# Seven half-block products for the down projection of the third and fourth batches

## The chip, the cores and the metric

The kernel runs on one core of one Trainium2 chip. The metric is the device time of one execution in microseconds (us). Before the change the median of three runs is 677.57 us (676.94 to 678.1). The program has the core's five engines: PE (TensorE, matrix products), DVE (VectorE), ACT (ScalarE), POOL (GpSimd) and SP (SyncE, which issues the transfers).

## The reference

Four batches go through a local attention with block summaries, and then through a mixer over tokens and channels. Cut to what matters:

```
attn: 4 batches, 8 heads, 768 tokens, 64 per head; softmax over a window of 16
      around each token and over 24 block maxima, times values and block means
x  = attention output, 768 tokens x 512 channels per batch
u  = x + (x^T U V)^T                    # token mixing, rank 32
ch = max(u @ w_ch1, 0) @ w_ch2          # 512 -> 2048 -> 512
return u + ch                           # float32
```

The change concerns `@ w_ch2`, called *down* below; `@ w_ch1` is called *up*.

## The kernel before

**Accuracy by parts.** Every factor of a large product is split into a high part (a cast by ACT) and a low part (value minus high part, by DVE or POOL); the function `split` does both. A product is then three matmuls: high by high, high by low, low by high.

**Batches.** The first batch is computed together with the preparation of the weights, by a list written out by hand. For the later three batches the kernel walks up and then down. Up is done by seven products of half blocks in place of eight (Strassen's scheme, in Winograd's form): the channels, the hidden units and the tokens are halved, sums of the weight blocks lie ready in memory (`up_there`), sums of the token blocks are made by `operands`, and `up_phase` makes, for each of 8 pairs of hidden blocks, seven products of 6 matmuls with 384 columns. Down is plain: `down_phase` goes over 16 hidden blocks `f`, and for each over 6 token tiles `t`, with three matmuls of 512 columns. There the activations are the stationary operand, so the result comes out in token rows and is added to `st.x`; later `finish` turns it by 24 transposes per batch into channel rows, which are what is stored.

**The work beside the products.** `gates` makes the high part (ACT, with the relu) and the low part (DVE, line 1136) of the 768 tokens of a hidden block, one block ahead. Weights come from memory whole: `fetch_weight` loads 512 KB at a time into a ring of three buffers, and `prepare` makes a *unit* of it, ACT the high part (line 184) and POOL the low part (line 185), into a ring of eight. About four units are ready ahead of their use. `tick` counts the steps until the next load, and `drip` issues small sums for the attention's block means.

**The order.** Each engine runs its instructions in the order in which the Python code emits them. The loop at the end of the body emits, after each step of up or down, the next pieces of the attention of the following batch (`later_steps`, spread evenly by `spread`), the finishing of the batch before (`finish`), a load when one is due, and a drip. In a step of up there are 6 matmuls, in a step of down 3.

Of the kernel before, what the change touches and what calls it, by code (L numbers as in the profile page):

```python
# [10 lines left out]
F32 = mybir.dt.float32  # L11
# [7 lines left out]
P = 128  # L19
# [25 lines left out]
BLOCKS = ("A11", "A12", "S2", "S1", "S3", "S4", "A22")  # L45
OPS = ("B11", "B21", "B22", "T1", "T2", "T3", "T4")
# [38 lines left out]
def body(ctx: ExitStack, tc, q0, q1, k, v, vn, uv, w1, w2, mask, ident, rep, out):  # L85
# [28 lines left out]
    def hidden_place(k, dt=F32):  # L114
        return wt.tile([P, 4 * NH], dt, name="place", tag=f"h{k}")
# [121 lines left out]
    def load_vsum(st, g, i):  # L237
# [4 lines left out]
        if st.b == 1 or st.b == 2 and g == 0:  # L242
            spare = hidden_place(2 + i)
        st.vn[g, i] = []
        for j in range(parts):
            if st.b == 0:
                t = vn0[g, i]
            elif spare is not None:
                t = spare[:, j * n : (j + 1) * n]
            else:  # L250
                t = mo.tile([P, DM], F32, name="stage", tag="val", bufs=VALS)[:, :n]
# [332 lines left out]
    def mix_u_out(st, hf, c):  # L584
        if hf not in st.u:
            st.u[hf] = [
                hidden_place(4 + 2 * hf + i, F32R).rearrange("p (c q) -> p c q", q=NH) for i in range(2)
# [3 lines left out]
        nc.scalar.copy(uh[:, c, :], ps[:, :NH])  # L591
        nc.vector.tensor_tensor(ul[:, c, :], ps[:, :NH], f32(uh)[:, c, :], ALU.subtract)  # L592
# [21 lines left out]

    def operands(st, i, k):

        if not st.op:
            for j, name in enumerate(OPS):
                t = wt.tile([P, 4 * NH], F32R, name="op", tag=f"op{j}")
                st.op[name] = t.rearrange("p (s i q) -> p s i q", s=2, q=NH)  # L620
        ps = turn_tokens(st, k < 2, 2 * i + k % 2)

        def part(name, val):
            t = st.op[name][:, :, i]
# [4 lines left out]

        if k == 0:  # L630
            st.tmp["T1"] = tmp()
            nc.scalar.copy(st.tmp["T1"], ps)
        elif k == 1:
            part("B22", ps)
            st.tmp["T3"] = tmp()
            nc.vector.tensor_tensor(st.tmp["T3"], ps, st.tmp["T1"], ALU.subtract)
            part("T3", st.tmp["T3"])
        elif k == 2:
            part("B11", ps)
            st.tmp["T2"] = tmp()  # L640
            nc.vector.tensor_tensor(st.tmp["T1"], st.tmp["T1"], ps, ALU.subtract)
            nc.vector.tensor_tensor(st.tmp["T2"], st.tmp["T3"], ps, ALU.add)
            part("T1", st.tmp["T1"])
            part("T2", st.tmp["T2"])
        else:
            part("B21", ps)
            nc.vector.tensor_tensor(st.tmp["T3"], ps, st.tmp["T2"], ALU.subtract)
            part("T4", st.tmp["T3"])
# [50 lines left out]
    down_there = [dram.tile([P, 2, DM], F32, name=f"down{p}", bufs=1) for p in range(NF // 2)]  # L699
# [608 lines left out]
```

## Time and profile before

The profiled execution took 678.02 us, of which 676.2 us lie between its first and last instruction (the span). The times are in us; each row is a stretch of the span. "Up" and "down" are those of the second, third and fourth batch.

| stretch | what | length | PE busy | DVE | ACT | POOL |
|---|---|---|---|---|---|---|
| 0 to 234 | first batch, weights, attention of the second | 234.0 | 208.7 | 176.1 | 117.6 | 157.1 |
| 234 to 306.5 | second, up | 72.5 | 70.7 | 45.4 | 45.9 | 45.8 |
| 306.5 to 386.5 | second, down | 80.0 | 79.1 | 45.3 | 35.7 | 31.8 |
| 386.5 to 462 | third, up | 75.5 | 74.9 | 40.2 | 50.7 | 50.8 |
| 462 to 542 | third, down | 80.0 | 79.1 | 43.3 | 35.7 | 27.6 |
| 542 to 601 | fourth, up | 59.0 | 59.0 | 15.5 | 34.1 | 37.9 |
| 601 to 669.3 | fourth, down | 68.3 | 68.3 | 20.6 | 20.3 | 21.1 |
| 669.3 to 676.2 | end: transposes, copies, stores | 6.9 | 2.2 | 0.4 | 3.2 | 0 |

A busy PE is a PE with a matmul in its pipeline. A recorded duration of an instruction on DVE or POOL contains what it waited inside the instruction. Rows of the timeline read: start, duration, engine, line, operation, output and inputs, shapes, count.

### The profile page before, as it was taken

What the parts mean: (1) busy time and instruction counts of PE and PEld (TensorE: products, weight loads), DVE (VectorE), ACT (ScalarE), POOL (GpSimd) and SP (SyncE); (2) the same over time, 40 slices, a digit from 0 to 9 for tenths busy, and PEclk for the clock granted to TensorE, in tenths of its full rate; (3) what the DMA queues carried; (4) which work ended last, traced back from release to release, by engine and by line L of the source; (5) the groups of instructions that cost most, each with busy time, mean ns of one, the idle gap of its engine ahead of it and who ended that gap; (6) DMA issues with size and microseconds to landing.
All of it is one profiled execution on the core that took longest, in us unless ns stands there. A gap on an engine that the chain in (4) does not pass through costs nothing.

```text
span 676.2 us, 13190 instructions
## 1 busy us (share of the span) xinstructions
PE 641.9 (95%) x4800; PEld 568.2 (84%) x4800; DVE 386.6 (57%) x1041; ACT 343.1 (51%) x751; POOL 372.0 (55%) x428
## 2 busy tenths in 40 slices
PE   5889997989999899999999999999999999999997
PEld 4768796879888799998877899998877899998886
DVE  3778798777898666555655634566654432232222
ACT  3855356355433556665453467665543365553322
POOL 5846967635697757651245486661334375563420
PEclk9999999899999999999999999999999999999999
DMA  9999679898992169785438059777432144431002
GB/s 250 249 345 279 218 231 297 252 272 305 279 330 100 52 185 309 209 250 151 143 104 248 23 174 311 229 222 220 127 97 79 55 148 165 139 126 62 32 0 94
DMA packets 82752, 124.47 MB, mean 184 GB/s; under 512 B 7680, under 2 KB 57728, under 8 KB 82688
## 3 DMA queue, kind: packets, MB, share of 16 engines
q1 hardware_dynamic: 82688, 123.63, 60.3%
q8 instruction: 38, 0.62, 0.4%
q14 instruction: 26, 0.21, 0.1%
HBM read 96.34 MB, written 27.26 MB: 183 GB/s over the span
## 4 chain that ended last, share of the span: by engine, by line
PE 75%; DMA 11%; DVE 6%; ACT 3%; SPq 2%; POOL 2%; issue 1%; ACTq 0%; POOLq 0%; DVEq 0%
PE acc L1151 27%; PE ps_h L1066 24%; PE acc L813 7%; PE ps_h L791 6%; PE ps_s L321 4%; PE ps_x L423 3%; DMA place<-in_q 2%; DMA qz<-in_q 2%; PE ps_o L610 2%; DMA place<-in_w 1%; DMA at<-there 1%; DMA place<-in_v 1%; DVE gl L1136 1%; DMA kt<-in_k 1%; DMA place<-in_k 1%
## 5 line engine op out<-in xcount | busy, mean ns | idle before, releaser
L185 POOL TENSOR_TENSOR parts<-whole,parts 128x512 fp32r<-128x512 f32 (+1 forms) x144 | 181.6, 1270 | 165.6 <-ACT parts L184 137.1
L1151 PE MATMUL acc<-parts,gh 128*128 128x512 f32 x576 | 193.4, 399 | 0.0
L1066 PE MATMUL ps_h<-op,parts 128*128 128x384 f32 x1008 | 188.4, 339 | 1.2 <-POOL parts L185 0.6
L1066 PEld LDWEIGHTS ps_h<-op,parts 128*128 128x128 f32 x1008 | 173.6, 188 | 3.1 <-POOL parts L185 0.9
L1151 PEld LDWEIGHTS acc<-parts,gh 128*128 128x128 f32 x576 | 108.1, 188 | 22.9 <-issue 0.8
L1151 PE MATMUL acc<-parts,gl 128*128 128x512 f32 x288 | 113.1, 393 | 1.9 <-DVE gl L1136 1.9
L1136 DVE SCALAR_TENSOR_TENSOR gl<-place,gh 128x768 fp32r<-128x768 f32 x48 | 58.9, 1228 | 83.1 <-ACT gh L1135 83.0
L184 ACT CAST parts<-whole 128x512 fp32r<-128x512 f32 (+1 forms) x144 | 83.5, 583 | 5.8 <-DMA whole<-up 4.3
L351 ACT ACTIVATE e<-e,neg 128x120 f32<-128x120 f32 x144 | 46.5, 386 | 59.7 <-DVE neg L341 53.6
L791 PE MATMUL ps_h<-place 128*128 128x384 f32 x384 | 74.3, 341 | 1.2 <-DVE place L592 0.5
L813 PE MATMUL acc<-place,gh 128*128 128x512 f32 x192 | 68.3, 411 | 2.1 <-POOL place L185 2.1
L791 PEld LDWEIGHTS ps_h<-place 128*128 128x128 f32 x384 | 66.6, 188 | 4.2 <-DVE place L592 1.3
L1135 ACT ACTIVATE gh<-place 128x768 fp32r<-128x768 f32 x48 | 40.6, 846 | 55.1 <-PE acc L1151 54.9
L1151 PEld LDWEIGHTS acc<-parts,gl 128*128 128x128 f32 x288 | 54.2, 188 | 13.1 <-DVE gl L1136 3.9
L160 POOL TENSOR_SCALAR val<-place 128x512 f32<-128x512 f32 (+1 forms) x30 | 48.7, 1638 | 29.6 <-ACT place L147 17.7
L185 POOL TENSOR_TENSOR place<-val,place 128x512 fp32r<-128x512 f32 x29 | 38.6, 1351 | 19.5 <-ACT place L184 19.5
L185 POOL TENSOR_TENSOR op<-tmp,op 128x384 fp32r<-128x384 f32 x24 | 24.5, 1030 | 42.7 <-ACT op L184 38.5
L341 DVE CUSTOM_DVE_ANT_0 e<-ps_s,mask_sb 128x120 f32<-128x120 f32 x144 | 32.9, 278 | 25.3 <-PE ps_s L321 24.5
L813 PEld LDWEIGHTS acc<-place,gh 128*128 128x128 f32 x192 | 36.6, 192 | 11.1 <-POOL place L185 3.4
L803 ACT ACTIVATE gh<-ps_h 128x384 fp32r<-128x384 f32 x32 | 15.6, 488 | 54.3 <-PE ps_h L791 54.1
L321 PEld LDWEIGHTS ps_s<-kt,qz 128*128 128x128 f32 x288 | 39.0, 191 | 4.4 <-DVE kt L303 1.6
L321 PE MATMUL ps_s<-kt,qz 128*128 128x120 f32 x288 | 39.7, 274 | 2.0 <-DVE kt L303 1.2
(110 smaller groups left out, 848.4 us busy)
## 6 DMA issues: line engine op xcount, KB each, us to landing
place<-in_w SPq DMA_DIRECT2D x32, 512.0 KB, 6.0
whole<-up SPq DMA_DIRECT2D x24, 512.0 KB, 4.0
whole<-down SPq DMA_DIRECT2D x24, 512.0 KB, 3.7
there<-squares SPq DMA_DIRECT2D x24, 384.0 KB, 4.2
at<-there SPq DMA_DIRECT2D x96, 96.0 KB, 3.9
whole<-up SPq DMA_DIRECT2D x24, 384.0 KB, 3.5
vt<-in_v SPq DMA_DIRECT2D x48, 146.2 KB, 4.0
kt<-in_k SPq DMA_DIRECT2D x24, 288.0 KB, 5.6
```

Of the source, the lines that this page charges most:

```text
L160: nc.gpsimd.tensor_scalar(f32(bits), f32(hi), 0.0, None, ALU.mult)
L184: nc.scalar.copy(hi, val)
L185: engine.tensor_tensor(lo, val, f32(hi), ALU.subtract)
L321: nc.tensor.matmul(ps[:, i * KC : (i + 1) * KC], qt[:, 64 + j * P : 64 + j * P + P], kt[:, k0 : k0 + KC], start=True, stop=True,)
L341: nc.vector.tensor_tensor_reduce(out=e[:, i, :], in0=ps[:, i * KC : (i + 1) * KC], in1=mask_sb[:, m, :], scale=-SCALE, scalar=BIG, op0=ALU ...
L351: nc.scalar.activation(e[:, i, :], e[:, i, :], AF.Exp, bias=st.neg[h][:, u : u + 1], scale=-1.0,)
L791: nc.tensor.matmul(ps[:, :NH], w_split[0, f][:, c % 2, part_w, c // 2], ut[:, c, :], start=(n == 0), stop=(n == 3 * NC - 1),)
L813: nc.tensor.matmul(acc[t], gt[:, sl], w_split[1, f][:, part_w], start=(first and j == 0), stop=(last and j == 2),)
L1066: nc.tensor.matmul(ps, a[:, sa, i], b[:, sb, i], start=(first and n == 0), stop=(n == 5), skip_group_check=not first,)
L1135: nc.scalar.activation(gh, h, AF.Relu)
L1136: nc.vector.scalar_tensor_tensor(gl, h, 0.0, f32(gh), ALU.max, ALU.subtract)
L1151: nc.tensor.matmul(acc[t], gt[:, sl], w[:, part_w], start=(f == 0 and j == 0), stop=(f == NF - 1 and j == 2),)
```

## The change

For the third and fourth batches (`st.b >= STRASSEN`, which is 2) down is done by seven products as well. `down_products` takes the products one after the other, each over all 8 pairs of hidden blocks: 56 steps of 6 matmuls with 384 columns. The weights are now the stationary operand, so the result comes out in channel rows; `sum_out` adds it on DVE to what is already there, and stores it. There is no `finish` for these batches; `operands` copies the turned tokens back into `st.x` (ACT), so that the mixed input stands in channel rows too.

The seven products need sums of activation blocks. Part of them is made in `up_phase` (one more relu on ACT and one more operation on DVE per pair), part in `part_steps`, which for each of the 56 steps makes the sum if there is one (DVE), the high part (ACT) and the low part (DVE, or POOL for some steps). It runs 7 steps ahead of the products. The sums of the down weights are made once, in the second batch's down, by `sum_down` (two operations on POOL and two on DVE for each of 8 pairs, and two stores), and loaded from `sums_there`. The third and fourth batches load 14 times 512 KB for down in place of 8 times, and prepare 28 units in place of 16.

The attention pieces move: 20 in place of 15 of the third batch's are issued in the second batch's up, the rest in the first 66 steps of its down; the fourth batch's first 8 steps are issued at the end of the second batch's down, the others in the third batch's up. Loads for the block means of the fourth batch start earlier. The sums of up weights of the first batch lie in two buffers and are stored in two transfers in place of one.

```
+PRODUCTS = (("A11", "x"), ("S1", "y"), ("S2", "x"), ("S4", "y"), ("S3", "x"), ("A12", "z"), ("A22", "x"))
+BLOCK_OF = (((0, 0),), ((1, 1),), ((0, 1),), ((0, 1),), ((1, 1),), ((0, 0),), ((1, 0),))
+STRASSEN = 2
...
+    def sum_down(p, whole):
...
+        yield nc.gpsimd.tensor_tensor(s12[:, 0], a21, a22, ALU.add)
+        yield nc.gpsimd.tensor_tensor(s12[:, 1], s12[:, 0], a11, ALU.subtract)
+        yield nc.vector.tensor_tensor(s34[:, 0], a11, a21, ALU.subtract)
+        yield nc.vector.tensor_tensor(s34[:, 1], a12, s12[:, 1], ALU.subtract)
+        yield
+        yield
+        yield nc.sync.dma_start(out=sums_there[:, :2, p], in_=s12)
+        yield nc.sync.dma_start(out=sums_there[:, 2:, p], in_=s34)
...
+    def part_steps(st, parts, n):
...
+        if n < steps:
+            j, b11, t1, b21, b22 = blocks(n)
+            if j == 2:
+                nc.vector.scalar_tensor_tensor(t1, b22, 0.0, t1, ALU.max, ALU.subtract)
+            elif j == 3:
+                nc.vector.tensor_tensor(b11, t1, b11, ALU.subtract)
+            elif j == 6:
+                nc.vector.scalar_tensor_tensor(b21, b21, 0.0, t1, ALU.max, ALU.subtract)
+        if 1 <= n <= steps:
...
+            if j in (3, 5):
+                nc.scalar.activation(hi, val, AF.Relu)
+            else:
+                nc.scalar.copy(hi, val)
...
+        if 2 <= n <= steps + 1:
...
+            if j in (3, 5):
+                nc.vector.scalar_tensor_tensor(lo, val, 0.0, f32(hi), ALU.max, ALU.subtract)
+            else:
+                engine = nc.gpsimd if n % 4 == 2 and (n < 24 or st.b == B - 1) else nc.vector
+                engine.tensor_tensor(lo, val, f32(hi), ALU.subtract)
+
+    def sum_out(st, j, i, ps):
...
+        u = channels_of(st, n, c)
+        if j < 3:
+            nc.vector.tensor_tensor(u, u, by_tiles(ps), ALU.add)
+            return
+        o = mo.tile([P, DM], F32, name="o", tag="val", bufs=VALS)[:, :NH]
+        nc.vector.tensor_tensor(by_tiles(o), u, by_tiles(ps), ALU.add)
+        t0 = st.b * S + n * NH
+        nc.sync.dma_start(out=out[c, :, t0 : t0 + NH], in_=o)
+
+    def down_products(st, parts):
...
+            for sa, sb in ((0, 0), (0, 1), (1, 0)):
+                for i in range(2):
+                    col = n % 2 * 2 * P + i * P
+                    nc.tensor.matmul(
+                        banks[name][i],
+                        w[:, sa, col : col + P],
+                        g[sb],
...
+            for _ in range(2):
+                if ahead <= n + LEAD:
+                    part_steps(st, parts, ahead)
+                    ahead += 1
+            if outs:
+                sum_out(*outs.pop(0))
+            if p == NF // 2 - 1:
+                outs = [(st, j, i, banks[name][i]) for i in range(2)]
+            if n % 2 == 1:
+                prepare()
+            yield
...
+    LEAD, FIRST_PARTS = 7, 5
...
-    do(behind)
```

On the engines the change shows at two places. The first is DVE in the fourth batch's down. Before (line 1136 is the low part of a gate; line 1092, 1126 are sums of up; line 1159 adds a result to the tokens; one row for 14 blocks):

```order
L1136 SCALAR_TENSOR_TENSOR gl<-place,gh 128x768
L1092 TENSOR_TENSOR place<-place,ps_h 128x384
L1126 TENSOR_TENSOR place<-place,ps_h 128x384
L1136 SCALAR_TENSOR_TENSOR gl<-place,gh 128x768
L1092 TENSOR_TENSOR place<-place,ps_h 128x384
L1136 SCALAR_TENSOR_TENSOR gl<-place,gh 128x768 x14
L1159 TENSOR_TENSOR x<-x,acc_7189 128x512
```

In the changed kernel, from the end of its second product on (line 1301 adds a product's result, line 1274 makes a sum of activation blocks, lines 1293 and 1290 make the low parts; `place` are the activation blocks, `op`, `gh` and `gl` the parts):

```order
L1301 TENSOR_TENSOR x_5194<-x_5194,accy0_7641 128x3x128
L1274 TENSOR_TENSOR place_6961<-place_6962,place_6961 128x384
L1293 TENSOR_TENSOR op_7745<-place_7379,op_7745 128x384
L1301 TENSOR_TENSOR x_5194<-x_5194,accy1_7642 128x3x128
L1274 TENSOR_TENSOR place_7016<-place_7017,place_7016 128x384
L1293 TENSOR_TENSOR op_7745<-place_7451,op_7745 128x384
L1274 TENSOR_TENSOR place_7090<-place_7091,place_7090 128x384
L1290 SCALAR_TENSOR_TENSOR gh_7769<-place_6961,gh_7769 128x384
L1274 TENSOR_TENSOR place_7162<-place_7163,place_7162 128x384
L1290 SCALAR_TENSOR_TENSOR gl_7781<-place_7016,gl_7781 128x384
```

Where one operation of 768 columns stood for each of 16 blocks, two of 384 columns stand for each step in such a stretch, and one elsewhere.

The second place is POOL in the third batch's down. Before (line 185 is the low part: `parts` of a weight unit, `op` of the next batch's token sums; `e` is a buffer of the attention):

```order
L336 MEMSET e_6010 128x8
L185 TENSOR_TENSOR parts_6034<-whole_5710,parts_6034 128x512
L185 TENSOR_TENSOR parts_6077<-whole_5777,parts_6077 128x512
L185 TENSOR_TENSOR parts_6146<-whole_5777,parts_6146 128x512
L185 TENSOR_TENSOR op_6138<-tmp_6189,op_6138 128x384
L185 TENSOR_TENSOR parts_6193<-whole_5970,parts_6193 128x512
L185 TENSOR_TENSOR op_6136<-tmp_6144,op_6136 128x384
```

In the changed kernel, from the start of that down (line 195 is `split`, line 1293 the low part of a step's activations):

```order
L1293 TENSOR_TENSOR gh_6130<-place_5025,gh_6130 128x384
L195 TENSOR_TENSOR parts_6150<-whole_6043,parts_6150 128x512
L195 TENSOR_TENSOR parts_6168<-whole_6043,parts_6168 128x512
L1293 TENSOR_TENSOR op_6184<-place_5624,op_6184 128x384
L195 TENSOR_TENSOR parts_6207<-whole_6102,parts_6207 128x512
L1293 TENSOR_TENSOR gh_6216<-place_5026,gh_6216 128x384
L195 TENSOR_TENSOR parts_6238<-whole_6102,parts_6238 128x512
```

One low part of activations now stands for every two units in the first product's steps, and there are 28 units in that down in place of 16.

More of the change, by code (lines that the diff above doesn't have):

```diff
@@ L768, in prepare @@
         prepared.append((key, t))
+        sums = second and key[0] == "down" and n < PER_BATCH
+        if sums:
+            stages.append(sum_down(key[1] // 2, fetched[n // 2]))
         if second:
-            due.append(4)
+            due.append(8 if sums else 4)
     def tick():
@@ L777, in tick @@
             fetch_weight()
+        if stages and next(stages[0], stages) is stages:
+            stages.pop(0)
     def use_weight(*key):
@@ L1186, in body @@
         cur, ahead, after = ([*sts, None, None][b + i] for i in range(3))
-        todo = later_steps(ahead) if ahead else []
-        mine, theirs = todo[:FIRST_STEPS], todo[FIRST_STEPS:]
-        steps = spread(mine, 4, UP)
-        ends = spread(behind, 2, 2 + 2 * len(behind))
+        new = b >= STRASSEN
+        todo = later_steps(ahead) if ahead and not new else []
+        if ahead and new:
+            steps = spread([(later_step, ahead, i) for i in range(EARLY, STEPS)], 9, UP)
+        else:
+            steps = spread(todo[:FIRST_STEPS], 4, UP)
+        ends = spread(behind, 2 - new, 2 - new + (2 - new) * len(behind))
         phase = up_phase(cur)
+        g = {}
         for i in itertools.count():
```

224 lines of the change are left out of this document (168 added, 56 removed).

## The prediction, made before the changed kernel ran

> **What bounds the kernel now.** I read the page first, then the busy times by stretch, then the chain of work that ended last. Page, busy times; and by stretch (length, then PE, PEld, DVE, ACT, POOL busy, with counts):
>
> ```profile
> PE 641.9 (95%) x4800; PEld 568.2 (84%) x4800; DVE 386.6 (57%) x1041; ACT 343.1 (51%) x751; POOL 372.0 (55%) x428
> ```
> ```profile
> 462.00:542.00 80.00, 79.07 (x632) 63.53 (x631) 43.30 (x92) 35.69 (x70) 27.58 (x24) 1.00 0.34 102
> 542.00:601.00 59.00, 59.00 (x350) 58.70 (x349) 15.45 (x27) 34.12 (x72) 37.87 (x34) 1.00 0.47 147
> 601.00:669.30 68.30, 68.30 (x307) 56.66 (x306) 20.59 (x25) 20.25 (x31) 21.13 (x14) 1.00 0.11 39
> 669.30:676.20 6.90, 2.24 (x21) 2.00 (x19) 0.35 (x1) 3.15 (x8) 0.00 (x0) 0.97 0.63 228
> ```
>
> PE is the bound of both changed stages: 79.07 of 80 us and 68.30 of 68.30, at a granted clock of 1.00, with DVE and POOL at a third. The waits of PE say the same; the only one in a later down is
>
> ```profile
> PE acc L1151 <- DVE gl L1136: 1.9, 4, 0.6
> ```
>
> The chain in order of time gives the pace of each kind of matmul where nothing interrupts it:
>
> ```profile
> 562.75 38.50 PE ps_h L1066 x222
> ...
> 606.32 62.61 PE acc L1151 x276
> ```
>
> A 384-column matmul takes 38.50/222 = 0.1734 us, a 512-column one 62.61/276 = 0.2268 us.
>
> **The change, part by part.** *Matmuls of down.* Before, 16 x 6 x 3 = 288 of 512 columns: 65.3 us. After, 7 x 8 x 6 = 336 of 384 columns: 58.3 us. Gain 7.05 us per batch, 14.1 for two. [...]
>
> *Transposes.* The finish of the third batch stood in the fourth's up (timeline):
>
> ```profile
> 545.50 2.35 PE L1066 MATMUL ps_h<-op,parts 128*128 128x384 f32 x12
> 547.68 0.49 PE L610 MATMUL ps_o<-ident_sb,x 128*128 128x128 f32 x3
> 547.93 2.33 PE L1066 MATMUL ps_h<-op,parts 128*128 128x384 f32 x12
> ```
>
> From 545.50 to 547.93 is 2.43 us, less 12 x 0.1734 = 2.08: three transposes cost 0.35. Eight such groups: gain 2.8.
>
> *The end.* Before, transposes, eight copies and stores followed the last product:
>
> ```profile
> 668.53 0.39 PE L1151 MATMUL acc<-parts,gh 128*128 128x512 f32 x1
> ...
> 669.29 3.16 ACT L1167 COPY o<-ps_o 128x384 f32<-128x384 f32 x8 [7.64 <-PE ps_o L610]
> 669.79 3.79 SPq L1169 DMA_DIRECT2D out_t<-o  x8
> ```
>
> That is 676.2 - 668.9 = 7.3 us. After, two DVE adds (about 0.55 + 0.47) and a store; the last copy here ended 3.75 before the end with a queue of issues, so a store costs 2.2 (its median landing) to 3.75, and I take 3.1. Gain 7.3 - 4.1 = 3.2. The three gains make 20.1.
>
> *DVE and POOL.* The price stands here. The low part of a gate has two inputs in SBUF, and so has every POOL subtraction. DVE (timeline):
>
> ```profile
> 345.12 1.85 DVE L1136 SCALAR_TENSOR_TENSOR gl<-place,gh 128x768 fp32r<-128x768 f32 x1 [1.85 <-ACT gh L1135]
> 346.89 0.55 DVE L185 TENSOR_TENSOR op<-ps_o,op 128x384 fp32r<-128x384 f32 x1
> 347.36 0.54 DVE L641 TENSOR_TENSOR tmp<-tmp,ps_o 128x384 f32<-128x384 f32 x1
> ...
> 355.30 1.88 DVE L1136 SCALAR_TENSOR_TENSOR gl<-place,gh 128x768 fp32r<-128x768 f32 x1 [1.85 <-ACT gh L1135]
> ```
> ```profile
> 612.72 0.96 DVE L1136 SCALAR_TENSOR_TENSOR gl<-place,gh 128x768 fp32r<-128x768 f32 x1 [3.14 <-ACT gh L1135]
> ```
>
> POOL (timeline):
>
> ```profile
> 344.87 1.28 POOL L185 TENSOR_TENSOR parts<-whole,parts 128x512 fp32r<-128x512 f32 x1
> ...
> 355.05 3.28 POOL L185 TENSOR_TENSOR parts<-whole,parts 128x512 fp32r<-128x512 f32 x2
> ```
> ```profile
> 613.27 1.55 POOL L185 TENSOR_TENSOR parts<-whole,parts 128x512 fp32r<-128x512 f32 x1 [2.54 <-ACT parts L184]
> ```
>
> The two take turns. At 345.12 DVE starts while POOL works, and ends 0.82 after POOL's end at 346.15, though alone it takes 0.96. At 613.27 POOL starts while DVE works and ends 1.14 after DVE. At 355 POOL, DVE, POOL run strictly in a row (ends at 356.33, 357.18, 358.33). Operations with one input in PSUM are not held up (line 1105 below, at most 555 ns). Single lines, min/median/max in ns:
>
> ```profile
> L838 DVE TENSOR_TENSOR o<-o,place x8: 557/559/1301, 230.6 to 245.8; 128x384 f32<-128x384 f32 x8
> ```
> ```profile
> L1105 DVE TENSOR_TENSOR place<-place,ps_h x24: 512/553/555, 235.3 to 596.2; 128x384 f32<-128x384 f32 x24
> ```
> ```profile
> L185 POOL TENSOR_TENSOR op<-tmp,op x24: 1006/1017/1322, 180.4 to 541.9; 128x384 fp32r<-128x384 f32 x24
> ```
>
> So a turn costs 1.14 for a POOL unit of 512, 0.87 (1.01 less the same 0.14) for POOL's 384, and for DVE's 384 between 0.43 (0.56 less 0.13) and 0.46 (next start after 346.89 in a row). [...]
>
> *Fourth batch's down.* A step of 6 matmuls is 1.04 us; PE alone needs 58.3 plus the 12 products left over from up (2.1) = 60.4. In two steps with no sum to make, the port carries two DVE low parts and one unit: 0.92 + 1.14 = 2.06 against 2.08. In the 24 of 56 steps for which line 1272, 1274 or 1276 makes a sum first, two steps carry 2.98. The lead of 7 steps (5 for the low part) is spent there. From the fourth step on DVE has 64 two-input operations, POOL 8 low parts and 23 units: 64 x 0.46 + 8 x 0.87 + 23 x 1.14 = 62.6. DVE's 13 adds from PSUM (0.47 each, 6.1) run partly under POOL's turns: half, 3.0. DVE can begin that work 3.2 us in (two steps before the fourth), and PE ends one step, 1.0, behind it: 3.2 + 62.6 + 3.0 + 1.0 = 69.8, a stall of 9.4. Lower bound (0.43 a turn, all adds hidden): 4.5. Upper (begin at 5.2, none hidden): 14.5. I take 9.4, the middle.
>
> *Third batch's down.* PE alone: 60.4 + 24 transposes of `operands` (2.8) + 12 matmuls of 256 columns (0.12 each, by the line through the two paces: 1.4) = 64.6. DVE has 68 turns, POOL 12 (8 of `operands`) and 23 units: 31.3 + 10.4 + 26.2 = 67.9. DVE's one-input operations: 13 adds, 14 of `operands`, 6 mixing adds of 0.68,
>
> ```profile
> L605 DVE TENSOR_TENSOR x<-x,ps_u x18: 648/683/689, 156.6 to 527.8; 128x512 f32<-128x512 f32 x18
> ```
>
> together 6.1 + 6.6 + 4.1 = 16.8; half 8.4. 3.2 + 67.9 + 8.4 + 1.0 = 80.5: a stall of 15.9, which I take, between 5.4 (0.43 a turn, all of it hidden) and 26.3 (begin at 5.2, none hidden). Behind a late low part PE holds up everything, the transposes of `operands` too; the token sums queued on DVE behind it are wanted only in the next up.
>
> *What is hidden.* ACT in that stage, by
>
> ```profile
> L184 ACT CAST parts<-whole 128x512 fp32r<-128x512 f32 x120 | 74.0, 619 | 5.8 <-DMA whole<-up 4.3 <-issue 0.5 <-PE ps_h L1066 0.3
> ...
> L184 ACT CAST op<-tmp 128x384 fp32r<-128x384 f32 x24 | 12.0, 514 | 23.8 <-DVE tmp L641 10.1 <-DVE tmp L647 7.0 <-DVE tmp L636 6.6
> ...
> L261 POOL TENSOR_TENSOR stage<-stage 128x256 f32<-128x256 f32 x12 | 8.9, 738 | 0.0
> ```
>
> 28 units x 0.62 + 78 of 384 columns (56 parts, 22 of `operands`) x 0.51 = 57.1, under PE's 64.6; without that cover 1 us per us. The loads land in
>
> ```profile
> whole<-down SPq DMA_DIRECT2D x24, 512.0 KB, 3.7
> ```
>
> against 6 steps (6.2 us) of notice. *Second batch's down* takes 16 sums on POOL (0.74 less 0.14: 9.6), 16 on DVE (0.46 at most: 7.4), and half a batch more of block means (about half of the 8.9 above): some 20 us more of the port. A gate's low part then waits one more POOL turn more often; before, four such waits made 1.9 in all. Between 0 and 5, I take 2. The denser attention in the third batch's up: 0 to 2, I take 0.5. The 16 extra stores and the split stores of the first batch ride on SP's queue: 0.
>
> *Sum*, against the profiled 678.0 (span 676.2 plus 1.8; 0.45 above the median): -20.1 + 9.4 + 15.9 + 2.5 = +7.7, so 685.7 profiled and 685.3 as a median. With all bounds low -20.1 + 4.5 + 5.4 = -10.2, with all high -20.1 + 14.5 + 26.3 + 7 = +27.7.
>
> **Rivals.** (1) *The port is crowded, but the gains win* (the other side). One mechanism: DVE's one-input work slips under POOL's turns and the leads take the rest, so the stalls are 13.5 and not 27.8; it decides once they stay under 20.1. For it: bounds 5.4 and 4.5; at 346.89 two such operations start back to back. Against: POOL's turns fill only half the time. 678.0 + (13.5 - 20.1) - 0.45 = 671. (2) *The port costs nothing that lasts*: PE stays the bound with only the 2.5 of the earlier stages, 660. For: PE waited 1.9 us in all for a low part. Against: 62.6 of turns in 60.4. (3) *SP's queue*: a result's store waits on SP for DVE's add, which lags up to 5 steps; the load behind it is late, and ACT's cast of that unit holds up the parts behind it. Three pairs of stores at about 2 us on top of the forecast: 691. Against: four units stand ready ahead.
>
> **How the numbers follow.** A measurement of this kernel tells about 0.2% (1.4 us) from no change. Forecast (slower by the port, 679 to 696): 0.43. Rival 3: 0.11. Between it and rival 1, within 0.2%: 0.08. Rival 1: 0.28. Rival 2: 0.10. So slower 0.54, same 0.08, faster 0.38. The range 667 to 697 leaves out rival 2 and the ends of the others, about 0.18; the forecast's own range is 679 to 696.
>
> **What would show it.** Right: PE busy well under its stretch in the third and fourth batches' down, waits of PE for line 1293 and 1290 on DVE, DVE and POOL rows stretched beyond 0.56 and 1.28, the stall greatest behind the steps that make sums (second to fourth product and sixth to seventh). Matmul pace 0.1734 and an end of about 4 us show the gains. Wrong: PE without gaps there (rival 2), waits for POOL units or for transfers (rival 3), or DVE rows at 0.56 while POOL works, which would take the port out of the account.

## The result, and the profile after

The changed kernel takes 719.5 us (median of 4 runs, 717.06 to 720.85), the kernel before beside it 677.84 (676.94 to 679.02): a ratio of 1.061, 95% interval 1.058 to 1.064. It is slower, as forecast, but by 42 us where 7.7 were forecast, and outside the range. The profiled execution took 720.24 us, its span is 718.3.

Busy times on the page of the changed kernel:

```profile
PE 644.3 (90%) x4848; PEld 581.2 (81%) x4848; DVE 522.4 (73%) x1201; ACT 382.9 (53%) x867; POOL 449.2 (63%) x484
```

PE is as busy as before, DVE has 136 us more, POOL 77. By stretch (length, then PE, PEld, DVE, ACT, POOL, granted clock, DMA share, GB/s); the six rows are up and down of the second, third and fourth batch, each cut where its first product starts (so they differ by up to 6 us from the stretches of the tables ahead), the last with the end:

```profile
230.90:312.30 81.40, 74.83 (x642) 72.37 (x641) 49.86 (x176) 47.40 (x113) 45.38 (x59) 0.98 0.77 227
312.30:407.30 95.00, 86.45 (x603) 68.28 (x602) 67.38 (x150) 45.47 (x96) 59.96 (x70) 1.00 0.61 178
407.30:495.30 88.00, 79.72 (x846) 75.45 (x845) 48.27 (x154) 53.73 (x128) 41.02 (x47) 0.96 0.69 208
495.30:582.60 87.30, 73.51 (x385) 67.02 (x385) 85.02 (x109) 48.38 (x106) 56.78 (x41) 0.94 0.29 90
582.60:638.80 56.20, 56.20 (x326) 56.20 (x325) 23.84 (x31) 33.48 (x72) 38.51 (x34) 1.00 0.48 150
638.80:718.30 79.50, 66.46 (x350) 60.93 (x348) 75.25 (x88) 38.55 (x81) 51.08 (x36) 0.97 0.29 93
```

In the two changed downs DVE is busy for 85.0 of 87.3 us and 75.3 of 79.5, and PE is not. But the stages ahead, which the forecast had nearly let alone, grew as well. The same cuts in every kernel that ran (us; "from second up" is the sum; the 224 to 234 us of the first batch ahead are left out):

| kernel | second up | second down | third up | third down | fourth up | fourth down, end | from second up |
|---|---|---|---|---|---|---|---|
| before | 69.9 | 85.8 | 69.8 | 85.9 | 59.0 | 75.1 | 445.5 |
| the change | 81.4 | 95.0 | 88.0 | 87.3 | 56.2 | 79.5 | 487.4 |
| a: no POOL low parts in the downs | 79.8 | 94.9 | 86.2 | 66.4 | 56.1 | 64.6 | 448.0 |
| b: those low parts on DVE | 81.9 | 95.0 | 86.3 | 77.8 | 56.2 | 67.6 | 464.8 |
| c: no sums of weights | 79.3 | 89.3 | 87.1 | 87.4 | 56.2 | 79.0 | 478.4 |
| d: sums not stored | 80.6 | 96.6 | 87.1 | 87.4 | 56.2 | 78.5 | 486.4 |
| e: moved attention alone | 80.3 | 88.5 | 82.6 | 73.2 | 59.0 | 75.2 | 458.8 |
| f: fetch ahead of send | 77.0 | 95.0 | 82.1 | 87.4 | 56.2 | 79.1 | 476.9 |
| g: fourth batch alone | 73.2 | 87.8 | 69.7 | 90.2 | 59.0 | 66.0 | 445.9 |
| h: b, f, sums on DVE | 79.8 | 95.4 | 81.7 | 78.3 | 56.2 | 66.1 | 457.4 |
| i: g, f, sums in the fourth's up | 71.3 | 86.0 | 69.7 | 87.0 | 62.1 | 66.0 | 442.1 |
| j: e and f | 81.0 | 88.6 | 83.1 | 73.2 | 59.0 | 75.2 | 460.1 |
| k: before and f | 70.7 | 85.9 | 69.7 | 85.9 | 59.0 | 75.2 | 446.3 |
| l: c, buffers held as with sums | 80.9 | 89.3 | 87.0 | 87.4 | 56.2 | 79.1 | 479.9 |
| m: sums, buffers held 5 steps | 81.6 | 101.0 | 88.3 | 87.4 | 56.2 | 79.1 | 493.5 |

Seven of these kernels have the same pieces in the second's up and the same order on SP's queue there (the change, a, b, c, d, l and m); theirs takes 79.3 to 81.9 us, so a difference of 2 us in such a stage tells little. Most kernels below ran once; the executions of the kernel before beside them lie between 675.1 and 683.2 us.

What the prediction named as signs is there. In the third batch's down PE waits for low parts from DVE (waits: us in total, times, longest):

```profile
PE accx L1325 <- DVE op L1293: 3.2, 3, 1.5
PE accy L1325 <- DVE gl L1290: 2.9, 2, 1.5
```

At the start of the fourth's down DVE and POOL go strictly in turns (timeline: start, duration, engine, line; ACT and SP left out):

```profile
639.91 3.19 POOL L195 TENSOR_TENSOR parts<-whole,parts 128x512 fp32r<-128x512 f32 x2
640.75 2.76 DVE L1293 TENSOR_TENSOR gl<-place,gl 128x384 fp32r<-128x384 f32 x2
...
643.06 1.34 POOL L1293 TENSOR_TENSOR op<-place,op 128x384 fp32r<-128x384 f32 x1
...
643.44 4.23 DVE L1293 TENSOR_TENSOR op<-place,op 128x384 fp32r<-128x384 f32 x3
...
644.35 1.60 POOL L195 TENSOR_TENSOR parts<-whole,parts 128x512 fp32r<-128x512 f32 x1
...
645.92 1.33 POOL L1293 TENSOR_TENSOR gh<-place,gh 128x384 fp32r<-128x384 f32 x1
```

Two POOL operations of 512 columns take 3.19 us, and three of DVE 4.23, beside POOL operations of 384, 512 and 384 columns: one of each per 1.4 to 1.6 us. A turn of each was put at 1.14 + 0.43 = 1.57, with POOL's 384 columns at 0.87 + 0.43 = 1.30. The price of a turn stands. What the prediction calls the port is the sum of such turns: the rows show that the two engines take turns, and not what makes them do so. The gains are there too: the pace of the products (from the chain) and the end (timeline).

```profile
582.81 53.99 PE ps_h L1137 x312
```
```profile
714.19 1.02 DVE L1304 TENSOR_TENSOR o<-x,accx 128x384 f32<-128x384 f32 x2 [1.13 <-PE accx L1325]
714.77 0.81 SPq L1306 DMA_DIRECT2D out_t<-o  x2
```

That is 0.173 us a matmul, and 718.3 - 714.2 = 4.1 from the start of the last two adds to the end.

### The profile page after: what moved, and what is told of

Read it like the earlier page. It is cut to its first block, busy times and chain, and to the rows that moved or that the text cites. A ratio compares the mean times of both kernels' runs of the same rounds, so it can differ in the third digit from the quotient of the medians.

```text
span 718.3 us, 13761 instructions
## 1 busy us (share of the span) xinstructions
PE 644.3 (90%) x4848; PEld 581.2 (81%) x4848; DVE 522.4 (73%) x1201; ACT 382.9 (53%) x867; POOL 449.2 (63%) x484
## 4 chain that ended last, share of the span: by engine, by line
PE 38%; DVE 28%; DMA 14%; issue 6%; ACT 5%; POOL 4%; SPq 4%; DVEq 0%; ACTq 0%; POOLq 0%
PE ps_h L1137 16%; PE acc L884 6%; PE ps_h L862 5%; DMA at<-there 4%; DMA whole<-up 3%; PE acc L1234 3%; DMA place<-in_v 3%; DVE op L1293 3%; PE ps_s L331 2%; DVE place L1274 2%; DMA qz<-in_q 2%; PE ps_x L433 2%; POOL parts L195 2%; DVE place L1272 2%; DVE place L1276 2%
## 5 line engine op out<-in xcount | busy, mean ns | idle before, releaser
L195 POOL TENSOR_TENSOR parts<-whole,parts 128x512 fp32r<-128x512 f32 (+1 forms) x168 | 218.8, 1314 | 139.5 <-ACT parts L194 124.8
L1137 PE MATMUL ps_h<-op,parts 128*128 128x384 f32 x1008 | 193.2, 344 | 1.8 <-ACT place L1208 1.8
L1137 PEld LDWEIGHTS ps_h<-op,parts 128*128 128x128 f32 x1008 | 176.5, 191 | 4.7 <-ACT place L1208 2.5
L194 ACT CAST parts<-whole 128x512 fp32r<-128x512 f32 (+1 forms) x168 | 97.3, 586 | 14.6 <-DMA whole<-up 7.3
L361 ACT ACTIVATE e<-e,neg 128x120 f32<-128x120 f32 x144 | 46.4, 386 | 53.2 <-DVE neg L351 45.3
L1234 PE MATMUL acc<-parts,gh 128*128 128x512 f32 x192 | 67.0, 404 | 0.0
L1234 PEld LDWEIGHTS acc<-parts,gh 128*128 128x128 f32 x192 | 36.1, 188 | 7.4 <-issue 0.2
L1234 PE MATMUL acc<-parts,gl 128*128 128x512 f32 x96 | 38.1, 397 | 2.3 <-DVE gl L1219 2.3
L433 PEld LDWEIGHTS ps_x<-vt,at 120*32 120x32 f32 x1152 | 18.7, 114 | 25.4 <-issue 9.0
L433 PE MATMUL ps_x<-vt,at 120*32 120x65 f32 x1152 | 22.6, 229 | 18.1 <-DMA at<-there 14.0
L1219 DVE SCALAR_TENSOR_TENSOR gl<-place,gh 128x768 fp32r<-128x768 f32 x16 | 22.6, 1412 | 21.8 <-ACT gh L1218 21.7
```

The source lines that it names most:

```text
L194: nc.scalar.copy(hi, val)
L195: engine.tensor_tensor(lo, val, f32(hi), ALU.subtract)
L361: nc.scalar.activation(e[:, i, :], e[:, i, :], AF.Exp, bias=st.neg[h][:, u : u + 1], scale=-1.0,)
L433: nc.tensor.matmul(ps[32 * i : 32 * i + 32, u * DV : (u + 1) * DV], at[:KC, i, u], vt[u % 2][:, (u // 2) * 2 + (i // 2 + u) % 2], start=Tr ...
L1137: nc.tensor.matmul(ps, a[:, sa, i], b[:, sb, i], start=(first and n == 0), stop=(n == 5), skip_group_check=not first,)
L1219: nc.vector.scalar_tensor_tensor(gl, h, 0.0, f32(gh), ALU.max, ALU.subtract)
```

## The experiments

The theory after the result: the turns of DVE and POOL hold the two downs, as forecast, and three other things cost the rest: the sums of weights, the moved attention, and something in the third batch's up. Each got its own runs.

The expectations of runs a to d speak of stages in other cuts: their 99, 91 and 77 us are the 95.0, 87.3 and 79.5 of the table, and their 80 for the second's down before is its 85.8. So differences compare, and lengths do not.

### The turns in the two downs: a and b

Run a leaves POOL's low parts of the weights out of the third and fourth downs:

```
-        split(hi, lo, whole, nc.gpsimd)
+        if key[0] == "down" and n >= PER_BATCH:
+            nc.scalar.copy(hi, whole)
+        else:
+            split(hi, lo, whole, nc.gpsimd)
...
-                        w[:, sa, col : col + P],
+                        w[:, 0, col : col + P],
```

> The changed kernel without POOL's low parts of the weights of down in the third and fourth batches (that part of the computation is left out: PE takes the high part twice, so its work is the same). [...] Rival (DVE alone has too much to do, or ACT's high parts come too late): both stages stay within 3 us of 91 and 77, about 717. If the granted clock fell because of the stalls, it is back at 1.00 in both stages.

Measured: 682.3 us. The two stages, with the same columns as above:

```profile
493.50:559.90 66.40, 65.80 (x387) 64.36 (x386) 59.90 (x111) 48.07 (x106) 22.03 (x15) 1.00 0.38 113
616.00:680.60 64.60, 60.58 (x350) 60.26 (x348) 46.39 (x87) 38.39 (x81) 13.33 (x10) 0.99 0.36 113
```

The two fall by 20.9 and 14.9 us; from POOL's 23 turns of 1.14 us a batch, 19 to 25 and 13 to 16 had been worked out, and about 684 us for the kernel. PE is busy throughout: 65.8 of 66.4 us, and 60.6 and the end, at a clock of 1.00 and 0.99. The same DVE work takes 25.1 us less in the third down, 28.9 less in the fourth. The largest group of low parts in the fourth (busy us, mean ns), in the changed kernel and in run a:

```profile
L1293 DVE TENSOR_TENSOR op<-place,op 128x384 fp32r<-128x384 f32 x12 | 14.8, 1243 | 0.0
```
```profile
L1296 DVE TENSOR_TENSOR op<-place,op 128x384 fp32r<-128x384 f32 x12 | 8.8, 746 | 3.9 <-ACT op L1287 3.8
```

POOL's turns are what stalls PE there, and DVE alone is not too full (busy for 59.9 of 66.4 us and 46.4 of 64.6). What fails in part is DVE's rows, which had been put at 0.54 to 0.56 us: beside the POOL work that is left (13.3 us in the fourth) this group stays at 0.75.

Run b keeps all the work and gives it to one engine:

```
-        split(hi, lo, whole, nc.gpsimd)
+        split(hi, lo, whole, nc.vector if key[0] == "down" and n >= PER_BATCH else nc.gpsimd)
...
-                engine = nc.gpsimd if n % 4 == 2 and (n < 24 or st.b == B - 1) else nc.vector
-                engine.tensor_tensor(lo, val, f32(hi), ALU.subtract)
+                nc.vector.tensor_tensor(lo, val, f32(hi), ALU.subtract)
```

> The changed kernel with the same work, but all low parts of the third and fourth batches' down made by DVE, none by POOL. Theory (port): a POOL turn of 1.14 us becomes one of DVE of 0.46 x 512/384 = 0.61, so the fourth batch's port carries 72 x 0.46 + 23 x 0.61 + 6.1 of adds = 53, under PE's 60.4: 61 to 65 us in place of 77. In the third 33 + 14 + 16.8 = 64 against PE's 64.6: 66 to 74 in place of 91. The kernel about 719.5 - 33 = 687, between 680 and 694. Rival (DVE as an engine is the bound, 99% busy): 31 more operations on it make the fourth batch's down longer than 77 us, about 85, and the kernel about 735.

Measured: 698.0 us (694.74 to 701.81), 1.028 of before (1.021 to 1.035): 21 us faster than the change, though above the 680 to 694 expected.

```profile
493.50:571.40 77.90, 69.08 (x387) 63.68 (x386) 72.92 (x141) 48.29 (x106) 12.23 (x10) 1.00 0.33 99
627.50:695.10 67.60, 61.70 (x350) 60.13 (x348) 61.55 (x124) 38.33 (x81) 0.00 (x0) 0.99 0.35 109
```

More work on DVE, and both stages shorter, the fourth's by 11.9 us (12 to 16 expected): a unit's low part takes less time as DVE's operation (0.73 us, below) than as POOL's turn (1.14), and in the changed kernel, in the strict turns from 639.91 on, DVE's operations of 384 columns took 1.4 us each beside POOL's (4.23 for three). But the third falls by 9.5 us where 17 to 25 were expected: there DVE is busy for 72.9 of 77.9 us, and is now the bound itself. My sum had 23 operations of 512 columns at 0.61 us; the stage has 25 at 0.73:

```profile
L195 DVE TENSOR_TENSOR parts<-whole,parts 128x512 fp32r<-128x512 f32 x25 | 18.3, 732 | 4.0 <-ACT parts L194 3.9
```

### The sums of down weights: c, d, l and m

Run c makes no sums:

```
-        sums = second and key[0] == "down" and n < PER_BATCH
+        sums = False
```

> The changed kernel without the sums of down weights in the second batch: no operation, no store, and the load behind follows after 4 steps as before (left out: the sums; the third and fourth batches load plain blocks of the same size in their place). Theory: the sums make the second batch's down long, 99 to about 83 us (3 us above the 80 of the kernel before for attention steps that moved in), the kernel about 703. Rival (the moved attention steps cost it): 96 to 99, kernel about 718.

Run d makes them and stores nothing:

```
-        yield nc.sync.dma_start(out=sums_there[:, :2, p], in_=s12)
-        yield nc.sync.dma_start(out=sums_there[:, 2:, p], in_=s34)
+        yield
+        yield
```

> The changed kernel with the sums of down weights made, but not stored (left out: the two stores of each of the 8 pairs; the third and fourth batches load plain blocks of the same size in their place). Theory 1 (the port: POOL's and DVE's sums hold up the copies and low parts on DVE): the second batch's down stays at 94 to 99 us, the kernel at 714 to 719. Theory 2 (SP's queue: the stores wait for sums that are late, and the loads and stores behind them, of block means, keys and probabilities, wait too): it falls to 82 to 87, the kernel to about 704.

Measured: c 710.9 us, its second down 89.3; d 715.6, its second down 96.6. So the sums cost that stage 5.7 us (95.0 less 89.3), where c expected 16; what is left, 3.5 more than the 85.8 before, is close to the 3 expected of the moved attention. From the second up on, c gains 9.0, of which 2.1 lie in the second up, ahead of the first sum, within what that stage differs by anyway. The stores are not needed for the cost, by d. But d does not take SP's queue out of the account: there the load of the next weights, which overwrites what the sums read, waits on the queue for DVE's last sum, 53.6 us in 8 times (the change: 15.7 in 5). DVE's rows of that stage in the changed kernel (busy us, mean ns):

```profile
L313 DVE COPY kt<-km 64x48 f32<-64x48 f32 x18 | 8.4, 467 | 0.3
L775 DVE TENSOR_TENSOR wsum<-whole,wsum 128x256 f32<-128x256 f32 x8 | 6.6, 823 | 0.6 <-POOL wsum L773 0.6
...
L774 DVE TENSOR_TENSOR wsum<-whole 128x256 f32<-128x256 f32 x8 | 5.3, 662 | 0.1
```

The sums stand in DVE's order ahead of gates' low parts and attention pieces: 11.9 us there, what they waited included, where 7.4 were counted. Run h below makes all four sums on DVE, and its second down is no shorter (95.4). That left one other suspect: with a sum, the weight buffer is held 8 steps instead of 4, and the next load comes later. Run l makes no sums and keeps the longer hold; run m makes them and holds the buffer for 5 steps:

```
-        if sums:
-            stages.append(sum_down(key[1] // 2, fetched[n // 2]))
```
```
-            due.append(8 if sums else 4)
+            due.append(5 if sums else 4)
```

> As the run without sums of down weights (left out: the sums and their stores), but each load of the second batch's down still follows after 8 steps instead of 4, as it does with the sums. Theory 1 (the work of the sums costs the second's down, on whichever engine, because it stands ahead of the gates' low parts on DVE or holds the port): the stage stays at 89 us as without sums, the kernel at 709 to 712. Theory 2 (the buffers that are held longer cost it, since the loads come late; then it is no wonder that the engine of the sums made no difference): 94 to 96, the kernel 715 to 719.

> The changed kernel with the sums, with the load that follows a summed pair issued after 5 steps in place of 8, the earliest at which the sums have been emitted. Theory 1 (the work of the sums): the second's down stays at 94 to 97 us, or gets longer, since the load now waits on SP's queue for the sums. Theory 2 (the buffers held longer): 90 to 92.

Measured: l 709.9 us, second down 89.3, with the same busy times as c; m 725.2, second down 101.0. The stretch in l:

```profile
309.20:398.50 89.30, 85.57 (x603) 68.08 (x603) 55.86 (x134) 45.51 (x96) 46.16 (x55) 1.00 0.48 142
```

In l, holding the buffer cost nothing: 89.3 us with it and 89.3 without (c). Letting it go sooner, in m, cost 6.0 us: the loads there wait 56.3 us on SP's queue for the sums, in 8 times. The cost comes with the sums, on either engine. PE's waits in the second's down show where it arrives; three of the change's:

```profile
PE acc L1234 <- DVE gl L1219: 2.3, 3, 1.4
...
PE ps_x L433 <- DMA at<-there: 1.4, 1, 1.4
...
PE ps_o L625 <- DVE x L620: 0.7, 1, 0.7
```

In all they are 8.5 us, in run c 3.7. Of the 4.8 between them, 1.2 are for gates' low parts (2.3 and 1.1), 1.8 for attention pieces that come late from DVE, 1.4 for fetched probabilities. Whether these came late by DVE's order or by SP's queue, no run separates.

### The moved attention and SP's queue: e, f, j and k

Run e has every down as before and no sums, but the attention pieces placed as in the change; in the third's down, mixing and operands stand at the same share of the stage:

```
-STRASSEN = 2
+STRASSEN = 4
+MOVED = 2
...
-        todo = later_steps(ahead) if ahead and not new else []
-        if ahead and new:
+        moved = b >= MOVED
+        todo = later_steps(ahead) if ahead and not moved else []
+        if ahead and moved:
```

> The attention pieces moved as in the changed kernel (20 in the second batch's up, 8 of the fourth batch's at the end of the second's down, the other 24 in the third's up, mixing and operands in the third's down), but every down as in the kernel before, and no sums of down weights. Theory (the moved pieces crowd the two ups, whose transfers are dense already): the second's up and the third's up stay near the 81 and 88 us of the changed kernel, where they were 70 and 70 before; the third's down gets shorter by the pieces that left it, and the kernel takes 690 to 705. Rival (the ups got longer by the extra relu and sum of line 1165, or through the down products beside them): both within 3 us of 70 plus the PE work moved in (3 each), the kernel 677 to 683.

Measured: 691.0 us. Second up, third up, third down:

```profile
230.10:310.40 80.30, 74.61 (x642) 72.09 (x640) 49.79 (x176) 47.42 (x113) 43.70 (x57) 0.98 0.78 231
...
398.90:481.50 82.60, 77.23 (x846) 73.09 (x846) 42.52 (x147) 50.56 (x118) 40.53 (x46) 1.00 0.75 223
481.50:554.70 73.20, 72.20 (x338) 59.80 (x337) 34.26 (x42) 29.48 (x50) 32.99 (x25) 1.00 0.19 59
```

The third down gives up 12.7 us, the ups take 10.4 and 12.8 more, the second down 2.7: moving the pieces costs 13.3 us by itself, with not one product changed. The prediction had 0.5. Most of a stage's change is the PE work that came or went with the pieces; the cost is PE's idle time. Length less PE busy is 3.9 us more than before in the second up, 2.1 in the second down, 4.8 in the third up and 0.1 in the third down: 10.8 of the 13.3.

In the changed kernel PE waited for the probabilities that come back from memory (the whole execution; 8.3 of the 14.0 us are in the third's up):

```profile
PE ps_x L433 <- DMA at<-there: 14.0, 9, 4.0
```

On SP's queue, in the third's up, the send of the next head stands ahead of that fetch, and waits for DVE's transpose:

```profile
SPq L386 <- DVE squares L381: 16.1, 5, 4.6
```

Run f exchanges the two:

```
             if 2 <= h <= H + 1:
                 fetch_squares(st, h - 2)
+            if 1 <= h <= H:
+                send_squares(st, h - 1)
```

(the send stood ahead of the fetch). Runs j and k make the same exchange in e and in the kernel before.

> The changed kernel with two groups of transfers exchanged on SP's queue: the probabilities of one head are fetched back before those of the next head are sent (the send waits for DVE's transpose, and the fetch stood behind it). Theory (the fetch is late because the send ahead of it waits on the queue): PE's waits for the fetched probabilities, 14.0 us in 9 times, fall under 5, the third's up from 88 to 79 to 83 us, the kernel to 709 to 714. Rival (the transfer itself is slow under the traffic of the loads): waits and stage stay within 2 us, the kernel at 717 to 720.

> The run with the moved attention pieces alone (691.0 us), with the fetch ahead of the send on SP's queue. Theory (what the denser pieces cost is mostly the fetch that waits behind a send): PE's waits for fetched probabilities from 11.0 us under 5, the third's up from 82.5 to 76 to 79, the kernel 681 to 686. Rival (the density itself, loads and DVE, costs it): the third's up 81 or more, the kernel 688 to 692.

> The kernel before, with the fetch ahead of the send on SP's queue and nothing else changed. There PE waits 3.8 us in 2 times for fetched probabilities. Theory (the order on the queue costs only where the pieces are dense): within 2 us of the kernel before. Rival (it is a gain of its own): 4 us or more faster.

Measured: f 705.8 us, 13.7 less than the change, more than expected: third up 82.1 for 88.0, second up 77.0 for 81.4, and 3.8 in the first batch, though the wait fell to 6.3 and not under 5. In the third's up the wait falls from 8.3 to 1.4 us, and the 6.8 us at half clock behind it (last section) are gone: the stage's clock is 1.00, where the change has 0.96. PE's wait in f, in e and in j (whole executions), and two of j's waits in its third up:

```profile
PE ps_x L433 <- DMA at<-there: 6.3, 5, 2.2
```
```profile
PE ps_x L434 <- DMA at<-there: 11.0, 6, 4.3
```
```profile
PE ps_x L434 <- DMA at<-there: 4.4, 4, 1.6
```
```profile
PE ps_x L434 <- DVE place L1187: 1.8, 1, 1.8
PE ps_x L434 <- DMA at<-there: 1.4, 1, 1.4
```

In j the wait falls from 11.0 to 4.4 us as forecast, and the time does not: 690.2, third up 83.1, the rival's numbers. In that up the wait falls from 5.4 (e) to 1.4, but 2.9 us of other waits appear, 1.8 of them for DVE, and so do 3.4 us at half clock, with 1.5 us more of busy PE. A wait was taken away and others took its place, so my explanation of what the density costs fell; the rival's, loads and DVE, is not shown by that. What remains shown: the place of the pieces costs 13.3 us; 5.9 more in the third up of the change come from the fetch behind the send; what sets the 82 us of the third up in e, f and j is open.

Run k missed on the other side: 674.2 us, 0.994 of before (0.991 to 0.996), a gain of about 5 us that I had put at under 2. Its second to fourth batches are as before; the second's up begins at 225.9 instead of 230.7, so the gain is in the first batch. There the kernel before waits 3.7 us for fetched probabilities, until 117.7, and has 6.8 us at half clock from 116.0 on; in k the longest such wait is 0.9, and there is no half clock.

### Put together: g, h and i

Run h is b and f, with the operands of the third and fourth batch and the sums of weights on DVE too:

```
-            split(t[:, 0], t[:, 1], val, nc.vector if name[0] == "B" else nc.gpsimd)
+            split(t[:, 0], t[:, 1], val, nc.vector if name[0] == "B" or st.b >= STRASSEN else nc.gpsimd)
...
-        yield nc.gpsimd.tensor_tensor(s12[:, 0], a21, a22, ALU.add)
-        yield nc.gpsimd.tensor_tensor(s12[:, 1], s12[:, 0], a11, ALU.subtract)
+        yield nc.vector.tensor_tensor(s12[:, 0], a21, a22, ALU.add)
+        yield nc.vector.tensor_tensor(s12[:, 1], s12[:, 0], a11, ALU.subtract)
```

Run g does only the fourth batch by seven products, attention as before, low parts of that down on DVE, and the sums, on DVE, for even pairs in the second down and odd pairs in the third:

```
-STRASSEN = 2
+STRASSEN = 3
...
-    FIRST_STEPS = 20
+    FIRST_STEPS = 15
...
+        sums = second and key[0] == "down" and n < 2 * PER_BATCH and key[1] // 2 % 2 == n // PER_BATCH
...
+            steps = spread(todo[FIRST_STEPS:], 0, DOWN - 5)
```

> Only the fourth batch's down by seven products, the third's plain; the attention pieces where they were before; all low parts in the fourth's down on DVE; the sums of down weights all on DVE, for half of the pairs in the second batch's down and for half in the third's. By the stages so far: the fourth's down and end 67.6 where the kernel before has 75.1, so -7.5; the sums 9 us at most where they cost what they did, 2 if DVE makes them alone in gaps: the kernel takes 671 to 677, faster than before. Rival (DVE's two-input work is what costs, wherever it stands): 678 to 684.

> [...] Theory (a POOL turn costs the port more than the same work on DVE; the fetch is late by the queue): second's down 95 to 89 to 92, third's up 86 to 80, third's down 78 to 73 to 76, the kernel 682 to 690. Rival (DVE itself is full): the second's down 95 or longer, third's down 80, the kernel 695 to 700.

Measured: g 677.3 us (672.47 to 681.38), 0.996 of before (0.993 to 0.999), between its forecast and the rival's; h 687.9, 1.014 (1.011 to 1.017). h gains in the third up what f gained, and the whole lies where it was expected; but its second down (95.4) and its third (78.3) are the rival's. In the third,

```profile
485.20:563.50 78.30, 69.05 (x386) 63.64 (x386) 74.72 (x149) 48.29 (x106) 2.60 (x2) 1.00 0.33 99
```

POOL does nothing and DVE is busy for 74.7 of 78.3 us. The rival "DVE itself is full" holds there, and not in the fourth. g's fourth down gains 9.1, and its sums give back 2.0 in the second down and 4.3 in the third; its second up was 3.3 longer in the profiled execution, the slowest of its ten, and that was not followed up. So run i makes the sums in the fourth's up, where no attention is left: each pair is loaded once more, six steps later summed on DVE, and stored; and it has f's exchange.

```
+            if new and i % SUM_EVERY == 0 and i // SUM_EVERY < NF // 2:
+                stages.append(sum_down(i // SUM_EVERY))
```

> As the run with only the fourth batch's down by seven products, but the sums of down weights are made in the fourth batch's up, where DVE is busy for 15 of 59 us and no attention is left: the 8 pairs are loaded once more, summed by DVE and stored; and the fetch of the probabilities stands ahead of the send. Theory (the sums cost where DVE and the queue serve attention and gates, and nothing where they do not): the second's down back to 86, the third's down from 90 to 86, the fourth's up stays at 59 to 60, the kernel 668 to 674. Rival (the added loads and sums hold up the fourth's up as they did the downs): fourth's up 63 or longer, the kernel 675 to 680.

Measured: 668.8 us (667.75 to 671.66), 0.986 of before (0.983 to 0.990): 1.4% shorter than the kernel before, and 7% shorter than the change. Its fourth up and fourth down:

```profile
538.10:600.20 62.10, 59.84 (x349) 58.60 (x348) 42.48 (x69) 37.72 (x83) 36.95 (x31) 1.00 0.80 267
600.20:666.20 66.00, 61.69 (x350) 60.13 (x348) 61.55 (x124) 38.32 (x81) 0.00 (x0) 0.99 0.36 112
```

The sums cost 3.1 us in the fourth up, a little over the forecast, and the seven products gain 9.1 in the down. Some 5 us of the 10.7 are f's exchange alone (run k), so seven products for the fourth batch are worth about the other half; the stages of i and k, 442.1 and 446.3 us, make it 4.

## Why the prediction was wrong

| step | predicted | measured | by |
|---|---|---|---|
| gains (products, transposes, end) | -20.1 | -20.2 | e and a: third down 73.2 to 66.4, fourth up 59.0 to 56.1, fourth down 75.1 to 64.6 |
| stall in the fourth's down | +9.4 (4.5 to 14.5) | +14.9 | the change against a: 79.5, 64.6 |
| stall in the third's down | +15.9 (5.4 to 26.3) | +20.9 | the change against a: 87.3, 66.4 |
| second's down, the sums | +2 (0 to 5) | +5.7 | the change against c and l: 95.0, 89.3 |
| denser attention | +0.5 (0 to 2) | +13.3 | e |
| stores on SP's queue, attention's queue order | 0 | about +7 | the rest, see below |
| sum | +7.7 | +41.9 | |

**The turns in the two downs and the gains were right.** The parts of the gain came out within 0.3 us (6.8 in the third's down, 2.9 in the fourth's up, 10.5 in the fourth's down); that their sum agrees to the tenth is luck. PE is busy for 65.8 and 60.6 us in run a, where 64.6 and 60.4 were worked out. The turns of the two engines were the right thing to sum, and a turn's price is what the timeline shows: 1.4 to 1.6 us for one of each, where 1.57 was worked out. That a port is behind them no run shows; the runs show the turns, and DVE's low parts at 1.24 us with POOL's work beside them and 0.75 without most of it (run a). The two stalls, 35.8 us, outweigh the gain of 20.2 without the other costs, so "slower" came from the turns that were summed, and the size did not.

**The step that failed most is "the denser attention in the third batch's up: 0 to 2, I take 0.5".** Moving the pieces cost 13.3 (run e): PE stood idle for 10.8 us more, in the second's up and down and in the third's up. The second's up, which takes 20 pieces in place of 15, had no term at all. I had priced the change's own operations and not the ones that it moves. The profile of before shows how different the two stages are, in its third up and third down (columns as above):

```profile
386.40:456.20 69.80, 69.19 (x554) 67.61 (x553) 36.48 (x132) 46.91 (x110) 48.83 (x65) 1.00 0.75 227
456.20:542.10 85.90, 84.97 (x665) 68.87 (x664) 47.18 (x108) 39.68 (x79) 29.73 (x27) 1.00 0.39 114
```

The pieces leave a stage with a DMA share of 0.39 for one with 0.75. I had read such rows for PE, DVE and POOL alone. That the transfers are what costs is not shown: run j's rows name waits for DVE too, and the cause of the 13.3 stays open. Another 5.4 us stand in the third's up of the changed kernel beside what e has (88.0, 82.6), and run f takes 5.9 off it: there SP's queue, past which I had moved transfers at 0, waited 16.1 us in 5 times for DVE's transpose, with the fetch behind. It is not rival 3's mechanism, a result's store ahead of a load, but the send of one head's probabilities ahead of the fetch of another's.

**The sums** were priced as turns of POOL that a gate's low part waits out. The gates' low parts take 1.41 us each there, and 1.38 in run l without the sums, and PE's wait for them grew by 1.2 us, within the term. Most of the rest of the 5.7 came by waits that it left out, for attention pieces and for probabilities, and the stage is as long with the sums on DVE alone (h, 95.4) as on both engines (95.0). Upper bound 5: it was made from the nearest wait that I knew, and not from the work added.

**The two stalls** are a size, not a mechanism. The fourth's is past its upper end, the third's in the upper half of its range. The sum took half of DVE's adds from PSUM as hidden under POOL's turns, and a full clock. In the fourth down DVE is busy for 75.3 of 79.5 us, so it looks nearer to the case "none hidden"; and the clock was not full (0.94 in the third's down and 0.97 in the fourth's; last section, at most 6 us for both stalls). How much is the one and how much the other no run separates.

**Rival 1** needed stalls under 20.1 in the two downs, and they had 35.8. **Rival 2** is excluded by run a.

## What to carry to other kernels

When a change moves work to make room, price the moved work in the stage that receives it, and ask there for every engine and queue that its pieces pass, before pricing the new work. Where a trace shows operations of DVE and POOL in turns, as here those with two operands in SBUF (from 639.91 on, one of each per 1.4 to 1.6 us), sum their turns on one clock; where that sum passed PE's time, giving the low parts to DVE was faster here (79.5 to 67.6, 87.3 to 77.8), until DVE's own total was the bound (72.9 of 77.9 us). Extra preparation belongs in the stage where no other work hangs on the same engine: the sums cost 5.7 us in the second batch's down and 3.1 in the fourth's up.

## What the runs showed that was not expected

PE was slowed twice by its stalls here. In the changed kernel the granted clock falls to one half (0.50) for 3.4 or 6.8 us after them (stretch, length, busy times as above, PEclk the third number from the right):

```profile
533.30:536.70 3.40, 1.32 (x6) 1.00 (x6) 3.40 (x3) 3.40 (x9) 3.40 (x3) 1.00 0.00 0
536.70:543.50 6.80, 5.22 (x16) 4.62 (x17) 6.80 (x8) 3.04 (x8) 4.94 (x4) 0.50 0.32 100
564.00:567.40 3.40, 1.43 (x7) 1.11 (x8) 3.40 (x5) 2.17 (x5) 2.82 (x2) 1.00 0.20 65
567.40:570.80 3.40, 3.40 (x11) 3.40 (x12) 3.40 (x8) 1.20 (x3) 0.61 (x1) 0.50 0.59 177
669.80:673.20 3.40, 1.32 (x7) 1.01 (x7) 3.40 (x5) 2.40 (x6) 3.40 (x3) 1.00 0.31 66
673.20:676.60 3.40, 3.40 (x10) 3.16 (x11) 3.40 (x6) 1.44 (x3) 1.23 (x2) 0.50 0.54 189
```

And what it does to the products of an up, 12 of them on either side of such a stall (timeline):

```profile
425.95 2.33 PE L1137 MATMUL ps_h<-op,parts 128*128 128x384 f32 x12
432.32 1.53 PE L433 MATMUL ps_x<-vt,at 120*32 120x65 f32 x48 [4.04 <-DMA at<-there]
433.78 4.14 PE L1137 MATMUL ps_h<-op,parts 128*128 128x384 f32 x12
```

Between the start of the second up and the last 2 us, the changed kernel has 23.8 us at half clock, the kernel before none, run a 6.8 and run h 3.4. In the two downs of the change 16 + 11 + 10 = 37 matmuls (three of them transposes) fall into such stretches, each about 0.17 us longer: some 6 us of the two stalls at most, since part of it would have been waiting anyway. In the 3.40 us ahead of these stretches PE was not idle, but busy for 1.32, 1.43 and 1.32 us. Where the limit lies these rows do not tell: a stretch of the same kernel with 2.76 of 3.40 us busy (from 656.0) kept its clock (1.00). So in this kernel PE lost half its clock without a full stop ahead of it, and such stalls have to be priced with what followed them.
